# Two of the five passes of a weight conversion moved from VectorE to GpSimd, in a kernel of an mLSTM cell and a multiplicative feed-forward block

## Chip, cores, metric

One core of one Trainium2 chip. The metric is the time of one execution on the device in microseconds (us); of a kernel I give the median of its runs. All ratios below are of runs in the fast state; where a run fell in the slow state (a second state, with a time some per cent longer whatever the kernel) this is said.

## The reference, cut to what matters

```python
def _attn_ref(q, k, v, i_gate, f_gate, o_gate):      # batch 4, heads 8, seq 768, head_dim 40
    ...                                              # recurrent mLSTM cell, token by token
        C = f_stab[..] * C + i_stab[..] * einsum('bhd,bhe->bhde', vt, kt)
        h_tilde = einsum('bhde,bhe->bhd', C, qt)
        y[:, :, t] = o * h_tilde / maximum(abs(nq), 1.0)

def _moe_ref(x, w1, w2, w3, w_out):                  # 3072 tokens, d_model 320, d_ff 1024
    return (((x @ w1) * (x @ w2)) @ w3) @ w_out
```

The four weight matrices arrive as 64-bit floating-point numbers. The kernel loads them as pairs of 32-bit words and converts them itself on the way, while the cell runs. It folds `w3 @ w_out` into one matrix (`wp`, then `w3o`), for which each half of a 128-row block of `w3`, once converted, is transposed on VectorE.

## The kernel before

The main loop has 30 passes. Pass s computes chunk s of the cell, the `up` products (x times w1 and w2, tiles `pa` and `pb` in PSUM, the memory that TensorE writes to; their product, made by VectorE, is `ab`, which frees their bank of PSUM) of chunks already done, and later the `down` products (`po`). In the early passes it also converts weights. The parts that matter:

```python
    def to_f32(dst, raw):                       # one conversion: five passes on VectorE
        n = dst.shape[-1]                       # 512 columns, or 320 for w_out
        lo, hi = raw[:, :, 0], raw[:, :, 1]
        t = wst.tile([128, n], U32, name="ex", tag="ex", bufs=1)
        r = wst.tile([128, n], U32, name="ma", tag="ma", bufs=1)
        V = nc.vector
        V.tensor_scalar(out=t, in0=hi, scalar1=3, ... logical_shift_left)
        V.scalar_tensor_tensor(out=t, in0=hi, scalar=0x80000000, in1=t, ... and, or)
        V.tensor_scalar(out=r, in0=t, scalar1=0xFF800000, ... and)
        V.scalar_tensor_tensor(out=r.bitcast(FP), in0=lo, scalar=2.0 ** -52, in1=r.bitcast(FP), ... mult, mult)
        V.tensor_tensor(out=dst, in0=t.bitcast(FP), in1=r.bitcast(FP), op=OP.add)

    def twice(n):                               # the y copy: last columns of y, beside themselves
        nc.gpsimd.tensor_copy(out=y_t[n][:, DM:DM + REM], in_=y_t[n][:, KF * P:DM])

    def x_trans(n):                             # px: y transposed by TensorE, for up
        for cc in range(KF + 1):
            transpose(px[:, cc, :], y[:, cc * P:(cc + 1) * P])

    n_cvt = [2, 1, 1, 1, 2, 2, 3, 3, 3] + [2] * 7        # conversions of each pass
    for s in range(len(n_up)):
        ...
        if 0 <= s - 2 < NU:
            twice(s - 2)
        ...                                     # px, up, the cell (first VectorE instruction: L346), y
        for _ in range(n_cvt[s] if s < len(n_cvt) else 0):
            convert()                           # to_f32; for w3 also the VectorE transpose to w3T
```

Each engine works through its own list of instructions in order; the timelines below show it (a copy on GpSimd whose input is ready at 65.5 us runs at 74.18, after the four passes ahead of it in the list). A pass of the loop only says in which order they are issued.

## Time and profile before

| | before |
|---|---|
| median of 3 runs | 489.06 us (488.94 to 491.42) |
| profiled span | 486.4 us |
| TensorE, VectorE, ScalarE, GpSimd busy | 94%, 54%, 30%, 18% |
| mean granted TensorE clock (share of its full speed) | 0.98 |

In this document a **stretch** runs from one instruction L346 (L364 in the changed file) to the next, and has the number of the pass whose L346 ends it; stretch 5 (60.36 to 72.50 us) so holds the conversions that pass 4 issues. The prediction counts its steps this way too. It runs its step 7 up to the first `ab`, behind which TensorE resumes at 98.81 us ("15.0 today" after 83.82); its "step 8 … TensorE's 14 us" fits the time from there to the L346 at 113.04, and its step 9 runs from there (TensorE's wait for w3T ends at 128.59).

The timeline of GpSimd of the kernel before (start, length in us, engine, line, operation, output<-input, and in brackets the idle time before and who ended it):

```profile
63.94 0.47 POOL L305 TENSOR_TENSOR state<-state,decay 128x164 f32<-128x164 f32 x1
65.78 0.37 POOL L386 COPY y<-y 128x64 f32<-128x64 f32 x1 [1.38 <-DVE y L382]
73.50 0.46 POOL L305 TENSOR_TENSOR state<-state,decay 128x164 f32<-128x164 f32 x1 [7.35 <-DVE state L350]
```

GpSimd waits for y, copies its last columns at once, and then has nothing to do for 7.35 us. That gap is what the change wants to use. The groups of VectorE by shape (count, busy us, mean ns), for the two passes to be moved:

```profile
L188 DVE TENSOR_TENSOR w<-ex,ma 128x512 f32<-128x512 f32 x24 | 18.6, 777 | 0.7
L187 DVE SCALAR_TENSOR_TENSOR ma<-raw,ma 128x512 f32<-128x512 uint32 x24 | 17.6, 735 | 0.7
```

### The profile page before, as it was taken

What the parts mean: (1) busy time and instruction counts of PE and PEld (TensorE: products, weight loads), DVE (VectorE), ACT (ScalarE), POOL (GpSimd) and SP (SyncE); (2) the same over time, 40 slices, a digit from 0 to 9 for tenths busy, and PEclk for the clock granted to TensorE, in tenths of its full rate; (3) what the DMA queues carried; (4) which work ended last, traced back from release to release, by engine and by line L of the source; (5) the groups of instructions that cost most, each with busy time, mean ns of one, the idle gap of its engine ahead of it and who ended that gap; (6) DMA issues with size and microseconds to landing.
All of it is one profiled execution on the core that took longest, in us unless ns stands there. A gap on an engine that the chain in (4) does not pass through costs nothing.

```text
span 486.4 us, 13366 instructions
## 1 busy us (share of the span) xinstructions
PE 456.8 (94%) x5658; PEld 374.8 (77%) x5658; DVE 260.9 (54%) x526; ACT 146.6 (30%) x399; POOL 88.3 (18%) x165
## 2 busy tenths in 40 slices
PE   3879797989899999999999999999999998999997
PEld 2769696988687888888777787777877777778864
DVE  7797698999778878877460614515235033011110
ACT  3644453633442543434430312311101011011011
POOL 5431222711302321403220211101000000000000
PEclk9997998989999999999999999999999999999999
DMA  9999936789966847521551425234020000000001
GB/s 188 173 187 203 168 87 134 119 162 182 190 130 138 172 112 154 120 52 39 100 110 43 111 59 122 52 94 93 19 81 3 27 15 15 28 13 15 1 13 40
DMA packets 116187, 45.76 MB, mean 94 GB/s; under 512 B 96736, under 2 KB 107168, under 8 KB 116128
## 3 DMA queue, kind: packets, MB, share of 16 engines
q1 hardware_dynamic: 112528, 40.88, 42.2%
q10 hardware_dynamic: 3600, 4.03, 2.4%
q8 instruction: 44, 0.72, 0.7%
q14 instruction: 15, 0.12, 0.1%
HBM read 40.86 MB, written 4.03 MB: 92 GB/s over the span
## 4 chain that ended last, share of the span: by engine, by line
PE 75%; DVE 8%; issue 8%; DMA 4%; SPq 2%; POOL 2%; ACT 1%; POOLq 0%; DVEq 0%
PE po L90 21%; PE pa L90 21%; PE pb L90 14%; PE cell L90 8%; PE wp L90 7%; PE pt L93 2%; DVE h L370 2%; PE px L93 1%; SPq L168 1%; DMA raw<-in_moe_w_dram 1%; DMA kbuf<-in_k_dram 1%; PE ub L90 1%; DMA raw<-in_moe_w_out_dram 1%; DVE o_in L380 1%; POOL pw L278 1%
## 5 line engine op out<-in xcount | busy, mean ns | idle before, releaser
L542 DVE TENSOR_TENSOR ab<-pb,a_sb 128x512 f32<-128x512 f32 x48 | 33.0, 690 | 162.9 <-ACT a_sb L541 162.7
L90 PE MATMUL po<-w3o,ab 128*128 128x320 f32 x384 | 105.4, 433 | 1.3 <-DVE h L370 1.3
L90 PEld LDWEIGHTS po<-w3o,ab 128*128 128x128 f32 x384 | 72.2, 190 | 30.7 <-issue 1.5
L90 PE MATMUL pa<-xT,w 128*128 128x256 f32 (+1 forms) x448 | 94.6, 360 | 0.6 <-ACT xT L396 0.6
L90 PE MATMUL pb<-xT,w 128*128 128x256 f32 (+1 forms) x448 | 91.7, 350 | 0.3 <-issue 0.3
L90 PEld LDWEIGHTS pa<-xT,w 128*128 128x128 f32 x448 | 78.6, 200 | 11.7 <-ACT xT L396 1.0
L90 PEld LDWEIGHTS pb<-xT,w 128*128 128x128 f32 x448 | 76.1, 191 | 8.4
L541 ACT ACTIVATE a_sb<-pa 128x512 f32<-128x512 f32 x48 | 28.6, 596 | 147.9 <-PE pb L90 147.9
L90 PE MATMUL pb<-xT,wr 64*64 64x256 f32 (+1 forms) x448 | 47.5, 352 | 0.0
L90 PE MATMUL pa<-xT,wr 64*64 64x256 f32 (+1 forms) x448 | 47.5, 352 | 0.0
L305 POOL TENSOR_TENSOR state<-state,decay 128x164 f32<-128x164 f32 x40 | 19.6, 493 | 148.4 <-PE cell L90 94.0
L278 POOL TENSOR_SCALAR_AFFINE_SELECT pw<-pw 64x512 f32<-64x512 f32 x48 | 36.8, 768 | 47.0 <-ACT pw L276 45.4
L276 ACT ACTIVATE pw<-pw,aT 128x64 f32<-128x64 f32 x160 | 40.6, 339 | 10.5 <-DMA pw<-U_d 10.5
L90 PEld LDWEIGHTS pa<-xT,wr 64*64 64x64 f32 x448 | 28.5, 133 | 14.9 <-issue 6.8
L90 PE MATMUL wp<-wo,w3T 128*128 128x320 f32 x128 | 35.9, 433 | 2.0 <-DVE w3T L237 2.0
L90 PEld LDWEIGHTS wp<-wo,w3T 128*128 128x128 f32 x128 | 23.7, 190 | 11.1 <-issue 2.2
L90 PEld LDWEIGHTS cell<-vbuf,pw 64*64 64x64 f32 x768 | 27.4, 141 | 4.2 <-issue 2.0
L549 ACT COPY o_sb<-po 128x320 f32<-128x320 f32 x24 | 10.2, 425 | 67.6 <-PE po L90 66.7
L90 PE MATMUL cell<-vbuf,pw 64*64 64x41 f32 x768 | 27.3, 230 | 1.4 <-issue 1.4
L90 PEld LDWEIGHTS pb<-xT,wr 64*64 64x64 f32 x448 | 28.5, 133 | 0.0
L386 POOL COPY y<-y 128x64 f32<-128x64 f32 x24 | 7.3, 302 | 109.9 <-DVE y L382 106.1
L346 DVE TENSOR_TENSOR pw<-cell,pw 128x512 f32<-128x512 f32 x24 | 16.4, 685 | 17.2 <-PE cell L90 13.6
(89 smaller groups left out, 514.3 us busy)
## 6 DMA issues: line engine op xcount, KB each, us to landing
raw<-in_moe_w_dram SPq DMA_DIRECT2D x64, 128.0 KB, 3.2
pw<-U_d SPq DMA_DIRECT2D x40, 128.0 KB, 3.6
kbuf<-in_k_dram SPq DMA_DIRECT2D x24, 160.0 KB, 4.5
vbuf<-in_v_dram SPq DMA_DIRECT2D x24, 160.0 KB, 4.9
o_in<-in_o_gate_dram SPq DMA_DIRECT2D x24, 160.0 KB, 3.9
out_dram<-o_sb ACTq DMA_DIRECT2D x24, 160.0 KB, 1.8
raw<-in_moe_w_dram SPq DMA_DIRECT2D x7, 512.0 KB, 6.0
qbuf<-in_q_dram SPq DMA_DIRECT2D x17, 160.0 KB, 5.1
```

Of the source, the lines that this page charges most:

```text
L90: in_order(nc.tensor.matmul(out, lhsT=lhsT, rhs=rhs, start=start, stop=stop))
L93: in_order(nc.tensor.transpose(out, in_, ident[0:n, 0:n]))
L168: nc.sync.dma_start(out=dst, in_=src)
L276: nc.scalar.activation(out=pw[:, h, :], in_=src[:, h, :], func=AF.Exp, bias=aT[:, c, b * H + h:b * H + h + 1])
L278: nc.gpsimd.affine_select(out=pw[r], in_=pw[r], compare_op=OP.is_ge, fill=0.0, base=0, pattern=[[0, H], [1, L]], channel_multiplier=-1)
L305: nc.gpsimd.tensor_tensor(out=new, in0=old, op=OP.mult, in1=decay[:, b * NP:(b + 1) * NP, 2 * c + x:2 * c + x + 1] .to_broadcast([P, NP, D1]))
L346: first_read = nc.vector.tensor_tensor(out=pv, in0=ss, in1=pv, op=OP.mult)
L370: nc.vector.tensor_tensor(out=h[r], in0=ph[x], in1=h[r], op=OP.add)
L386: nc.gpsimd.tensor_copy(out=y_t[n][:, DM:DM + REM], in_=y_t[n][:, KF * P:DM])
L541: nc.scalar.mul(out=a_sb, in_=pa, mul=UP ** -2)
L542: nc.vector.tensor_tensor(out=ab_t[gr][j][:, fs[0]:fs[-1] + 1, t0:t0 + a_sb.shape[-1]], in0=pb, in1=a_sb, op=OP.mult)
L549: nc.scalar.copy(out=o_sb, in_=po)
```

## The change

The intent: VectorE is about 90% busy in stretches 5 to 9 and GpSimd is not, so the multiply and the add that end a conversion go to GpSimd. The multiply on GpSimd is a plain one, so ScalarE scales the low words first. The scratch of such a conversion lies in `gates`, a tile that is free by then, one pair of columns for all. The transposes of w3 are put off to the next pass (`unturned`), so that VectorE needn't wait for GpSimd at once. Of the 34 conversions, the last two of each of passes 4 to 14 are changed, 22 in all.

```diff
-    def to_f32(dst, raw):
+    def to_f32(dst, raw, E=None):
...
+        if E is None:
+            t, r = (tiles "ex", "ma" as before)
+        else:
+            t, r = (gates[:, i * CW:i * CW + n].bitcast(U32) for i in range(2))
...
+        if E is None:
             V.scalar_tensor_tensor(out=r.bitcast(FP), in0=lo, scalar=2.0 ** -52, in1=r.bitcast(FP), op0=OP.mult, op1=OP.mult)
+        else:
+            V = E
+            nc.scalar.mul(out=lo.bitcast(FP), in_=lo, mul=2.0 ** -52)
+            V.tensor_tensor(out=r.bitcast(FP), in0=lo.bitcast(FP), in1=r.bitcast(FP), op=OP.mult)
         V.tensor_tensor(out=dst, in0=t.bitcast(FP), in1=r.bitcast(FP), op=OP.add)
...                                    # convert(): the transpose of w3 becomes turn_w3()
+        if E is None:
+            turn_w3(w3, ko, half)
+        else:
+            unturned.append((w3, ko, half))
...                                    # main loop
-            weighted(s)
-            if s >= B:
-                decayed(state[s % B][1], state[s % B][0], s, 0)
+            if s <= early:
+                weigh(s)
...
-        for _ in range(n_cvt[s] if s < len(n_cvt) else 0):
-            convert()
+        if early <= s < NU - 1:
+            weigh(s + 1)
+        while unturned:
+            turn_w3(*unturned.pop(0))
+        for i in range(n_cvt[s] if s < len(n_cvt) else 0):
+            convert(nc.gpsimd if i + 2 >= n_cvt[s] and early <= s < len(n_cvt) - 1 else None)
```

`early` is 4; `weigh` holds the two lines that were taken out above. In the changed file L184 to L186 are L187 to L189, the multiply is L191 on VectorE and L195 on GpSimd, the add L196, the scaling on ScalarE L194, the y copy L404, the transpose to w3T L254, `ab` L560.

More of the change, by code (lines that the diff above doesn't have):

```diff
@@ L173, in scale @@
         nc.scalar.mul(out=hi, in_=hi, mul=2.0 ** -111)
-    def to_f32(dst, raw):
+    def to_f32(dst, raw, E=None):
         n = dst.shape[-1]
         lo, hi = raw[:, :, 0], raw[:, :, 1]
-        t = wst.tile([128, n], U32, name="ex", tag="ex", bufs=1)
-        r = wst.tile([128, n], U32, name="ma", tag="ma", bufs=1)
+        if E is None:
+            t = wst.tile([128, n], U32, name="ex", tag="ex", bufs=1)
+            r = wst.tile([128, n], U32, name="ma", tag="ma", bufs=1)
+        else:
+            t, r = (gates[:, i * CW:i * CW + n].bitcast(U32) for i in range(2))
         V = nc.vector
@@ L186, in to_f32 @@
         V.tensor_scalar(out=r, in0=t, scalar1=0xFF800000, scalar2=None, op0=OP.bitwise_and)
-        V.scalar_tensor_tensor(out=r.bitcast(FP), in0=lo, scalar=2.0 ** -52, in1=r.bitcast(FP), op0=OP.mult, op1=OP.mult)
+        if E is None:
+            V.scalar_tensor_tensor(out=r.bitcast(FP), in0=lo, scalar=2.0 ** -52, in1=r.bitcast(FP), op0=OP.mult, op1=OP.mult)
+        else:
+            V = E
+            nc.scalar.mul(out=lo.bitcast(FP), in_=lo, mul=2.0 ** -52)
+            V.tensor_tensor(out=r.bitcast(FP), in0=lo.bitcast(FP), in1=r.bitcast(FP), op=OP.mult)
         V.tensor_tensor(out=dst, in0=t.bitcast(FP), in1=r.bitcast(FP), op=OP.add)
@@ L224, in scale_next, with convert @@
         scale(scaled[-1][1])
-    def convert():
+    def convert(E=None):
         if not scaled:
@@ L230, in convert, with turn_w3 @@
         if dst is not None:
-            to_f32(dst, raw)
+            to_f32(dst, raw, E)
             return
         w3 = wst.tile([128, CW], FP, name="w3", tag="w3")
-        to_f32(w3, raw)
-        if half == 0:
+        to_f32(w3, raw, E)
+        if ko not in w3T_t:
             w3T_t[ko] = wst.tile([128, FO, 128], FP, name="w3T", tag="w3T")
+        if E is None:
+            turn_w3(w3, ko, half)
+        else:
+            unturned.append((w3, ko, half))
+    unturned, halves_in = [], {}
+    def turn_w3(w3, ko, half):
         nc.vector.transpose(out=w3T_t[ko].rearrange("c k (m r) -> c m k r", r=32)[:, 2 * half:2 * half + 2],
                             in_=w3.rearrange("r (m k c) -> r m k c", m=2, k=FO))
-        if half:
+        halves_in[ko] = halves_in.get(ko, 0) + 1
+        if halves_in[ko] == 2:
             turned_w3.append(ko)
@@ L562, with weigh @@
     n_cvt = [2, 1, 1, 1, 2, 2, 3, 3, 3] + [2] * 7
-    pinned = 7
+    pinned, early = 7, 4
     behind = ExitStack()
     turned, converted, fetched = 0, 2, 2 * KF + 1
+    def weigh(n):
+        weighted(n)
+        if n >= B:
+            decayed(state[n % B][1], state[n % B][0], n, 0)
     for s in range(len(n_up)):
```

## The prediction

> **What bounds the kernel now.** A step is one pass of the main loop (s = 0 to 29). I read four views, from coarse to fine: the busy table and chain of the page, the stretch table cut at the starts of the step's first VectorE instruction (L346, `pw<-cell`), the waits of TensorE, and the timelines of the steps that the change touches.
>
> ```profile
> PE 456.8 (94%) x5658; PEld 374.8 (77%) x5658; DVE 260.9 (54%) x526; ACT 146.6 (30%) x399; POOL 88.3 (18%) x165
> ...
> PE 75%; DVE 8%; issue 8%; DMA 4%; SPq 2%; POOL 2%; ACT 1%; POOLq 0%; DVEq 0%
> ```
>
> TensorE is the bound on the whole and GpSimd is mostly idle. The averages hide two stages.
>
> ```profile
> 60.36:72.50 12.14, 12.14 (x227) 11.62 (x227) 10.95 (x22) 6.42 (x17) 3.25 (x6) 0.92 0.36 87
> 72.50:83.82 11.32, 8.02 (x184) 7.37 (x184) 10.12 (x23) 4.13 (x13) 3.25 (x6) 0.85 0.72 139
> 83.82:101.44 17.62, 15.36 (x285) 14.94 (x283) 16.06 (x34) 10.04 (x29) 8.97 (x14) 0.96 0.67 127
> 101.44:113.04 11.60, 11.60 (x251) 11.41 (x251) 10.74 (x26) 3.89 (x12) 3.65 (x6) 0.92 0.97 183
> 113.04:127.14 14.10, 13.57 (x214) 11.64 (x211) 13.11 (x28) 6.84 (x18) 2.64 (x5) 1.00 0.94 190
> 128.59:486.40 357.81, 352.86 (x3616) 278.81 (x3616) 153.44 (x304) 85.70 (x221) 43.37 (x75) 1.00 0.31 69
> ```
>
> The columns are length, then busy PE, PEld, DVE, ACT, POOL, then clock. The first five rows are steps 5 to 9: VectorE is busy about 90%, and it sets the pace together with TensorE. The last row is everything after: TensorE is busy without a break, VectorE 43%. The chain of waits says the same: from 128.59 us on it is nearly all matmuls. So VectorE time is worth something only before 128.6 us. A gain there is capped by what TensorE waits for:
>
> ```profile
> PE px L93 <- DVE y L382: 3.8, 2, 3.3
> PE cell L90 <- POOL vw L300: 2.6, 2, 1.9
> PE pt L93 <- DVE ab L542: 2.3, 1, 2.3
> PE wp L90 <- DVE w3T L237: 2.0, 1, 2.0
> ```
>
> Of these px, pt and wp, some 8 us or 1.6%, lie in the changed steps. A gain over 2% is therefore hardly possible.
>
> **What the Trainium skill says.** "GPSIMD Engine Reference", section "Performance versus the Vector engine", gives about 2.6 cycles per element at 1.2 GHz for a two-input operation on GpSimd and calls it about twice as slow as VectorE. The trace has two sizes of such an operation (with a broadcast second operand):
>
> ```profile
> 61.37 0.47 POOL L305 TENSOR_TENSOR state<-state,decay 128x164 f32<-128x164 f32 x1 [7.78 <-DVE state L350]
> 63.24 0.74 POOL L300 TENSOR_TENSOR vw<-vbuf,wT 128x328 f32<-128x328 f32 x1
> ```
>
> The columns are start and length in us: 0.47 and 0.74 us (465 and 737 ns as medians), a slope of 1.66 ns per element, so 1.04 us for 512 elements; the page's figure gives 1.1 us plus the 0.19 us intercept of my line, 1.3. I take 1.2 us for 128x512 and 0.8 us for 128x320, as estimates. "TensorE: Matmul & The Clock Gate", Part 1, says that an idle window of about 3.4 us halves the matmul clock until about 3.4 us of work have passed. The trace agrees: in step 6 TensorE waits 3.31 us for y and then runs at half clock:
>
> ```profile
> 79.50:80.50 1.00, 1.00 (x26) 0.50 0.00 0
> 80.50:81.50 1.00, 1.00 (x32) 0.50 0.28 77
> 81.50:82.50 1.00, 1.00 (x50) 0.50 0.62 183
> ```
>
> **The change part by part.** 22 of 34 conversions (the last two of each of steps 4 to 14, two being all there are except in steps 6 to 8) move their last two passes. VectorE loses 2 x 0.69 us for each 128x512 and 2 x 0.49 for each 128x320 one, about 28 us in all: plenty, but 12 x 1.38 = 17 us of it after step 9, where it has time anyway. ScalarE gains 22 scalings of the low words (0.68 or 0.50 us, some 14 us; it is 30% busy, so I charge nothing). GpSimd gains 44 operations, some 49 us on 88. The matmuls are the same, but the first product of w3 moves from step 10 to step 11 and step 17 does two.
>
> What decides is the order. Reading the built program with its semaphores, three things stand out.
> 1. The pair of scratch tiles (in `gates`) is single. The first VectorE pass of a step's second conversion waits for the GpSimd add of the first. VectorE then stands still, in order, where it used to go on.
> 2. GpSimd's small copy of y's last columns (L386 before) now stands behind both conversions of the step before. In steps 5 and 6, where one `up` is done, TensorE's px of the step needs that copy, and behind px stand the rest of `up` and all cell matmuls, in order.
> 3. From step 8 on px is of the y one step older, so the copy has a whole step of slack. But the transposes of w3 on VectorE wait for GpSimd's add, ahead of `ab`.
>
> Today the stretch that this lengthens is:
>
> ```profile
> 65.22 0.49 DVE L382 TENSOR_TENSOR y<-h,o_in 128x320 f32<-128x320 f32 x1
> 65.63 0.42 DVE L184 TENSOR_SCALAR ex<-raw 128x512 uint32<-128x512 uint32 x1
> ...
> 66.81 0.43 DVE L186 TENSOR_SCALAR ma<-ex 128x512 uint32<-128x512 uint32 x1
> 67.28 0.69 DVE L187 SCALAR_TENSOR_TENSOR ma<-raw,ma 128x512 f32<-128x512 uint32 x1
> ...
> 72.50 0.68 DVE L346 TENSOR_TENSOR pw<-cell,pw 128x512 f32<-128x512 f32 x1
> ```
>
> y is done at 65.71, the y copy at 66.15, px follows at once, and the cell matmuls end at 69.88; VectorE is the later one, with its two conversions until 71.86.
>
> Step 5, new: three passes until 67.24; GpSimd 2 x 1.2 until 69.7; three passes (1.55) until 71.3; GpSimd until 73.8; y copy 0.25, 74.1. TensorE has idled some 7.5 us and starts at half clock, so from the copy to the end of the cell matmuls I take what step 6 shows today in that state, 78.28 to 83.57, 5.3 us. L346 at 79.4 instead of 72.50: **+6.9**.
> Step 6, new: y is ready 5.35 us after L346, at 84.75; three passes, GpSimd 2.4, three passes of 128x320 (1.2), GpSimd 1.6, handovers 0.2: 91.7; copy, 91.95; 5.3 more: 97.25 instead of 83.82. A further **+6.5**.
> Step 7 needs no new px. From L346 to the first `ab` (which frees TensorE's PSUM bank): 5.35 + 2.5 (a whole conversion) + 1.2 + 1.65 (wait for GpSimd) + 1.2 + 1.2 + 0.65 = 13.75 us against 15.0 today: **-1.2**. Step 8 is then TensorE's 14 us as today.
> Step 9: VectorE from L346: y with three passes and a wait within, 7; wait and transpose, 1.5; three passes 1.6; GpSimd 2.5; transpose 0.7; two `ab` 1.4: 14.7 us, 2.2 more than TensorE's work, so TensorE resumes at 14.75 after the cell matmuls. Today it resumes at 15.8, after its wait of 2.0 for w3T, which is gone: **-1.1 to -1.3**, the product of w3 itself being paid later.
> From step 10 a step is 16.8 us of matmuls; VectorE needs some 14 and GpSimd 3.4 + 2 x 2.4 = 8.2, so nothing further. Sum: 6.9 + 6.5 - 1.2 - 1.3 = +10.9, **500.0 us**, 2.2% slower.
>
> **The rivals.** (a) The intended gain: VectorE's relief lets steps 5 to 9 shrink to TensorE's work, 3 to 8 us, 481 to 486 us. For it: VectorE is 90% busy there and L346 of step 5 comes 2.6 us after its matmuls. Against it: the two waits above are in the program, not guesses. (b) A wash: the early loss is smaller, because GpSimd takes 1.04 us or less and the clock falls for one step only; then the sum is +6 to +8, 495 to 497 us. For it: step 7 was stretched by DMA and GpSimd at the same time, and gives some back. (c) Worse: GpSimd and VectorE slow each other. Today L188 has a mean of 777 ns against a minimum of 678, L278 768 against 652. GpSimd at 1.5 us adds 0.3 to each of eight operations in steps 5 and 6, and its late release of raw buffers holds the queue of loads: 503 to 508.
>
> **Range and chances.** I take 500 us. The range 492 to 508 runs from the wash to the worse rival with one more us to spare at the low end for step 7. The 2% line is at 498.8, just under my value, so slower 0.55, same 0.42; faster 0.03, as even all the waits together hold no 2%.
>
> **What would show it.** Right: a TensorE wait `px <- POOL y` of some 7 us twice, near 66 to 74 and 84 to 92 us; clock near 0.5 after each; VectorE idle before the first pass of second conversions until GpSimd's add; L346 of step 6 near 97; the wait of wp for w3T gone; matmuls unbroken from about 140 us and then as today. Wrong: px starting without waiting on GpSimd, L346 of step 6 before 90 (GpSimd's passes well under 1 us, or y copied earlier), or new TensorE waits after step 10 (then slower still).

## The result, and the profile after

| | before | changed |
|---|---|---|
| median (runs of the same rounds) | 490.24 us (4 runs, 488.94 to 493.24) | 512.10 us (4 runs, 509.07 to 513.54) |
| ratio, 95% interval | | 1.0429 [1.0352, 1.0505] |
| profiled span | 486.4 us | 507.4 us |
| mean granted clock | 0.98 | 0.96 |

A ratio here is the mean time of one kernel's fast runs over that of the other's of the same rounds, so not quite the ratio of the medians. The change makes the kernel 4.3% slower: the direction was predicted, but the time is 4 us above the top of the range.

The busy times and the chain of work that ended last, from the page of the changed kernel:

```profile
PE 460.1 (91%) x5658; PEld 375.7 (74%) x5658; DVE 237.2 (47%) x482; ACT 158.4 (31%) x421; POOL 135.4 (27%) x209
...
PE 68%; POOL 5%; issue 5%; DVE 4%; DMA 2%; ACT 1%; SPq 1%; POOLq 0%; DVEq 0%; ACTq 0%
```

VectorE lost 23.7 us of work, GpSimd gained 47.1, as meant. But GpSimd's share of the chain rose from 2% to 5%. The stretches 5 to 9, in the order length, busy PE, PEld, DVE, ACT, POOL, clock:

```profile
60.19:79.88 19.69, 10.31 (x204) 9.62 (x204) 8.24 (x18) 5.27 (x16) 8.16 (x10) 0.74 0.64 115
79.88:99.75 19.87, 11.64 (x204) 10.90 (x204) 7.85 (x18) 7.52 (x21) 7.35 (x10) 0.71 0.45 81
99.75:118.00 18.25, 16.49 (x288) 15.82 (x289) 14.98 (x33) 12.46 (x39) 10.59 (x16) 0.94 0.40 83
118.00:130.97 12.97, 11.73 (x257) 11.07 (x255) 10.12 (x23) 5.49 (x13) 8.65 (x13) 1.00 0.94 187
130.97:145.43 14.46, 12.43 (x200) 10.50 (x201) 11.00 (x23) 5.08 (x14) 7.93 (x9) 1.00 0.83 173
```

In stretches 5 and 6 TensorE is busy for 52% and 59% of the time, and at a clock of 0.74 and 0.71. What it waits for (us in all, times, longest):

```profile
PE px L93 <- POOL y L404: 15.6, 2, 8.4
...
PE pt L93 <- DVE ab L560: 4.2, 5, 1.9
...
PE px L93 <- DVE y L400: 2.7, 3, 1.0
PE pa L90 <- DVE ab L560: 1.8, 2, 0.9
...
PE wp L90 <- DVE ab L560: 0.7, 1, 0.7
```

The wait of `wp` for w3T is gone, as predicted, and the one `px <- POOL y` is there twice, as predicted. Of the waits for `ab`, 6.7 us in all, the prediction had one, of 2.2 us in its step 9 (1.90 measured, below). The others were not predicted, and three of them (0.68, 0.62 and 0.29 us, at 177 to 212 us) lie after step 10, which the prediction named as a sign that it was wrong. GpSimd in stretch 5, which answers to the timeline shown of before:

```profile
67.20 1.29 POOL L195 TENSOR_TENSOR gates<-raw,gates 128x512 f32<-128x512 f32 x1 [2.97 <-issue]
68.56 1.26 POOL L196 TENSOR_TENSOR w<-gates 128x512 f32<-128x512 f32 x1
71.61 1.29 POOL L195 TENSOR_TENSOR gates<-raw,gates 128x512 f32<-128x512 f32 x1 [1.78 <-issue]
72.97 1.26 POOL L196 TENSOR_TENSOR w<-gates 128x512 f32<-128x512 f32 x1
74.18 0.24 POOL L404 COPY y<-y 128x64 f32<-128x64 f32 x1
```

y was done at 65.5 us (L400 on VectorE), and its copy starts at 74.18, where before it followed within 0.1 us: it stands behind four passes in GpSimd's list. Between the two conversions VectorE stands still as well, because there is one pair of scratch tiles (VectorE of the changed kernel):

```profile
66.64 0.43 DVE L189 TENSOR_SCALAR gates<-gates 128x512 uint32<-128x512 uint32 x1
69.86 0.43 DVE L187 TENSOR_SCALAR gates<-raw 128x512 uint32<-128x512 uint32 x1 [2.79 <-POOL w L196]
...
79.88 0.69 DVE L364 TENSOR_TENSOR pw<-cell,pw 128x512 f32<-128x512 f32 x1 [1.65 <-PE cell L90]
```

**Where the 21 us are.** Each row is the difference of the stretches' lengths between the two traces, taken from the starts of L346 and L364. From the end of stretch 17 (270.06 us before, 290.81 after) both kernels take 20.2 us a stretch.

| stretches | before | after | difference | predicted |
|---|---|---|---|---|
| start of stretch 5 | 60.36 | 60.19 | -0.17 | 0 |
| 5 | 12.14 | 19.69 | +7.55 | +6.9 |
| 6 | 11.32 | 19.87 | +8.55 | +6.5 |
| 7 and 8 | 29.22 | 31.22 | +2.00 | -1.2 |
| 9 to 17 | 157.02 | 159.84 | +2.82 | -1.3 |
| sum | | | +20.75 | +10.9 |

In the last row lies a shift that is no loss: the product of w3 of stretch 10 is done one stretch later, and so on until stretch 17 does two (260 matmuls instead of 244, 28.82 us instead of 24.51). The loss in it begins at the end of stretch 9 (VectorE of the changed kernel):

```profile
140.23 0.43 DVE L189 TENSOR_SCALAR gates<-gates 128x512 uint32<-128x512 uint32 x1
143.48 0.71 DVE L254 STREAM_TRANSPOSE w3T<-w 128x512 f32<-128x512 f32 x1 [2.82 <-POOL w L196]
144.22 1.29 DVE L560 TENSOR_TENSOR ab<-pb,a_sb 128x512 f32<-128x512 f32 x2
```

The second transpose of w3 waits 2.82 us for GpSimd's add, and `ab` stands behind it in VectorE's list. TensorE needs the PSUM bank that `ab` frees. It waits 1.90 us for it, where the prediction had 2.2, and then works at half clock, which the prediction didn't have (TensorE, then two slices of one microsecond with busy PE, PEld, DVE, ACT, POOL and clock):

```profile
144.97 0.66 PE L93 MATMUL pt<-ident,qbuf 128*128 128x128 f32 x4 [1.90 <-DVE ab L560]
```

```profile
147.00:148.00 1.00, 1.00 (x4) 0.82 (x3) 0.97 (x3) 1.00 (x3) 0.00 (x0) 0.50 0.82 240
148.00:149.00 1.00, 1.00 (x3) 0.80 (x3) 0.92 (x4) 0.85 (x2) 0.00 (x0) 0.50 0.47 121
```

This adds up. TensorE's idle time in stretches 9 to 13 is 0.53 + 1.89 = 2.42 us before and 2.03 + 0.68 + 0.62 + 0.30 = 3.63 us after (length minus busy in each stretch), 1.2 us more; the last three are again waits for `ab`. Stretch 10 has a mean clock of 0.89, so 0.11 x 15.32 = 1.7 us of it are lost to the clock. Together 2.9 us, against 2.82.

**GpSimd and VectorE get in each other's way.** In the same stretch two passes of VectorE that take 0.49 us elsewhere took 1.23 and 1.44 us, beside passes of GpSimd (VectorE, then GpSimd):

```profile
135.83 1.23 DVE L398 SCALAR_TENSOR_TENSOR o_in<-o_in,den 128x320 f32<-128x320 f32 x1
137.10 1.44 DVE L400 TENSOR_TENSOR y<-h,o_in 128x320 f32<-128x320 f32 x1
```

```profile
135.41 1.30 POOL L195 TENSOR_TENSOR gates<-raw,gates 128x512 f32<-128x512 f32 x1 [2.88 <-DMA raw<-in_moe_w_dram]
136.79 1.40 POOL L196 TENSOR_TENSOR w<-gates 128x512 f32<-128x512 f32 x1
```

Each of the two ends 0.35 us after the GpSimd pass beside it ends (137.06 against 136.71, 138.54 against 138.19). This is what the Trainium skill says in "SBUF — State Buffer", section "SBUF: two separate sides": VectorE's second pair of ports is shared with GpSimd as an exclusive lock, which a VectorE operation with two SBUF inputs and a GpSimd operation that reads SBUF take one after the other. The trace agrees; VectorE's two passes are 0.74 + 0.95 = 1.7 us longer here.

**Half clock lasts longer.** In stretch 6 the y copy ends at 92.98 us, and the cell matmuls at 99.68, 6.7 us later. The prediction took 5.3, from a stretch in which the half clock lasted some 3.4 us. Slices of the changed kernel:

```profile
93.00:94.00 1.00, 0.97 (x13) 0.74 (x17) 0.00 (x0) 0.45 (x1) 0.00 (x0) 0.50 1.29 227
...
97.00:98.00 1.00, 1.00 (x49) 1.00 (x46) 0.00 (x0) 1.00 (x6) 0.00 (x0) 0.50 1.01 208
...
101.00:102.00 1.00, 1.00 (x6) 1.00 (x5) 0.73 (x2) 0.73 (x2) 0.94 (x3) 0.51 0.00 0
102.00:103.00 1.00, 1.00 (x10) 1.00 (x10) 0.96 (x2) 1.00 (x5) 0.92 (x2) 1.00 0.00 0
```

TensorE is busy from 93.0 on, but the full clock comes back only at 102.0, after 9 us of work. In stretch 5 of the same kernel it came back after 3.6 us. Nor did the half clock always need the idle 3.4 us that the prediction took: it followed waits of TensorE of 1.90 us (above), of 2.26 us in the kernel before (98.81 us; clock 0.50 from 100 to 103) and of 1.98 us in e5 (129.72 us; 0.50 from 131 to 133), but not the wait of 1.98 us at 128.59 us in the kernel before (1.00 in the slices behind it). So none of the traces gives a fixed length of wait.

### The profile page after: what moved, and what is told of

It is laid out like the page before. It is cut to its first block, busy times and chain, and to the rows that moved or that the text cites. A ratio compares the mean times of both kernels' runs of the same rounds, so it can differ in the third digit from the quotient of the medians.

```text
span 507.4 us, 13428 instructions
## 1 busy us (share of the span) xinstructions
PE 460.1 (91%) x5658; PEld 375.7 (74%) x5658; DVE 237.2 (47%) x482; ACT 158.4 (31%) x421; POOL 135.4 (27%) x209
## 4 chain that ended last, share of the span: by engine, by line
PE 68%; POOL 5%; issue 5%; DVE 4%; DMA 2%; ACT 1%; SPq 1%; POOLq 0%; DVEq 0%; ACTq 0%
PE po L90 20%; PE pa L90 19%; PE pb L90 13%; PE cell L90 7%; PE wp L90 6%; POOL gates L195 2%; PE pt L93 2%; PE px L93 1%; DMA raw<-in_moe_w_out_dram 1%; DMA qbuf<-in_q_dram 1%; ACT pw L294 1%; POOL w L196 1%; SPq L168 1%; POOL pw L296 1%; DVE h L388 1%
## 5 line engine op out<-in xcount | busy, mean ns | idle before, releaser
L560 DVE TENSOR_TENSOR ab<-pb,a_sb 128x512 f32<-128x512 f32 x48 | 32.8, 689 | 168.9 <-ACT a_sb L559 168.6
L90 PE MATMUL pb<-xT,w 128*128 128x256 f32 (+1 forms) x448 | 92.8, 353 | 0.2 <-issue 0.2
L90 PEld LDWEIGHTS pb<-xT,w 128*128 128x128 f32 x448 | 77.3, 195 | 8.5
L323 POOL TENSOR_TENSOR state<-state,decay 128x164 f32<-128x164 f32 x40 | 19.2, 485 | 112.7 <-PE cell L90 65.5
L90 PE MATMUL pa<-xT,wr 64*64 64x256 f32 (+1 forms) x448 | 49.1, 362 | 0.0
L90 PE MATMUL pb<-xT,wr 64*64 64x256 f32 (+1 forms) x448 | 49.1, 362 | 0.0
L90 PEld LDWEIGHTS pa<-xT,wr 64*64 64x64 f32 x448 | 29.9, 139 | 15.1 <-issue 7.2
L195 POOL TENSOR_TENSOR gates<-raw,gates 128x512 f32<-128x512 f32 (+1 forms) x22 | 26.6, 1209 | 52.8 <-DVE gates L189 17.6
L296 POOL TENSOR_SCALAR_AFFINE_SELECT pw<-pw 64x512 f32<-64x512 f32 x48 | 33.3, 694 | 25.4 <-ACT pw L294 23.7
L93 PE MATMUL px<-ident,y 128*128 128x128 f32 x72 | 13.9, 295 | 18.3 <-POOL y L404 15.6
L90 PEld LDWEIGHTS pb<-xT,wr 64*64 64x64 f32 x448 | 29.9, 139 | 0.0
L404 POOL COPY y<-y 128x64 f32<-128x64 f32 x24 | 6.6, 275 | 86.8 <-DVE y L400 86.5
```

What stands on the lines that cost most here:

```text
L90: in_order(nc.tensor.matmul(out, lhsT=lhsT, rhs=rhs, start=start, stop=stop))
L93: in_order(nc.tensor.transpose(out, in_, ident[0:n, 0:n]))
L195: V.tensor_tensor(out=r.bitcast(FP), in0=lo.bitcast(FP), in1=r.bitcast(FP), op=OP.mult)
L296: nc.gpsimd.affine_select(out=pw[r], in_=pw[r], compare_op=OP.is_ge, fill=0.0, base=0, pattern=[[0, H], [1, L]], channel_multiplier=-1)
L323: nc.gpsimd.tensor_tensor(out=new, in0=old, op=OP.mult, in1=decay[:, b * NP:(b + 1) * NP, 2 * c + x:2 * c + x + 1] .to_broadcast([P, NP, D1]))
L560: nc.vector.tensor_tensor(out=ab_t[gr][j][:, fs[0]:fs[-1] + 1, t0:t0 + a_sb.shape[-1]], in0=pb, in1=a_sb, op=OP.mult)
```

## The experiments

The theory after reading the result: A, the y copy behind GpSimd's conversion passes makes most of the loss (stretches 5 and 6). Rivals and additions: B, the single pair of scratch tiles, which makes VectorE and GpSimd take turns; the order of the loop, which was changed as well; the half clock; and the transposes of w3 that wait for GpSimd ahead of `ab`. The expectations name theories by such letters; those of the last four runs are explained there. All twelve runs computed the right result.

| kernel | median us (runs) | ratio to before, 95% |
|---|---|---|
| changed | 512.10 (4) | 1.0429 [1.0352, 1.0505] |
| e1_ycopy | 498.85 (4) | 1.0197 [1.0113, 1.0281] |
| e2_scratch | 508.41 (4) | 1.0414 [1.0337, 1.0491] |
| e3_both | 497.07 (4) | 1.0180 [1.0105, 1.0254] |
| e4_none | 491.01 (4) | 1.0073 [0.9979, 1.0167] |
| e5_late | 495.85 (6) | 1.0110 [1.0080, 1.0141] |
| e6_warm | 509.41 (4) | 1.0396 [1.0354, 1.0439] |
| e7_no_w3 | 491.31 (6) | 1.0009 [0.9971, 1.0046] |
| e8_one_no_w3 | 491.14 (6) | 1.0007 [0.9976, 1.0038] |
| e9_both_gated | 490.24 (6) | 1.0025 [0.9968, 1.0083] |
| e10_late_gated | 489.72 (6) | 1.0044 [0.9962, 1.0126] |
| e11_vw_first | 490.23 (6) | 0.9997 [0.9939, 1.0054] |
| e12_one_gated | 494.65 (6) | 1.0109 [1.0059, 1.0158] |

The kernel before had medians of 489.0 to 490.8 us in these rounds, which ran on several chips; each ratio is to the kernel before of its own round. One run of it (493.15 us) and one of e11 were slow and are left out of the ratios.

### e1: the y copy ahead of the conversions

```diff
-        if 0 <= s - 2 < NU:
+        if 0 <= s - 2 < NU and (s - 2 < early - 1 or s - 1 > NU):
             twice(s - 2)
...
         if early <= s < NU - 1:
             weigh(s + 1)
+        if early <= s <= NU:
+            twice(s - 1)
```

> The changed kernel, but GpSimd's copy of y's last columns is issued ahead of the two conversions of its step instead of behind them. Theory A (the copy stuck behind the conversions makes most of the loss, through px and all that stands behind it on TensorE): the waits of px for GpSimd (8.4 and 7.2 us) go, step 5 and step 6 return to about 12 us each (19.7 and 19.9 in the changed kernel), VectorE's first instruction of step 6 starts near 84 to 86 us instead of 99.75, and the time falls by about 15 us to 493 to 498. Rival B (GpSimd's slow passes and the handovers with VectorE over the one pair of scratch tiles cost it, wherever the copy stands): steps 5 and 6 stay above 16 us and less than 6 us are saved.

Measured: 498.85 us, 1.0197. Stretches 5 and 6 are 11.96 and 12.64 us instead of 19.69 and 19.87, and no `px` waits for GpSimd any more. The time is 0.85 us above the expected range. GpSimd in stretch 5:

```profile
67.24 0.37 POOL L404 COPY y<-y 128x64 f32<-128x64 f32 x1 [1.38 <-DVE y L400]
68.84 1.30 POOL L195 TENSOR_TENSOR gates<-raw,gates 128x512 f32<-128x512 f32 x1 [1.23 <-DVE gates L189]
```

So the place of one instruction of 0.3 us in GpSimd's list makes more than half of the loss (1.0429 to 1.0197), as A said. The GpSimd passes themselves are as long as in the changed kernel, and stretch 5 is no longer than before the change (11.96 against 12.14 us).

### e2: a second pair of scratch tiles

```diff
-        if E is None:
+        if E is None or flip:                  # flip: the last conversion of a pass uses "ex", "ma"
             t = wst.tile([128, n], U32, name="ex", tag="ex", bufs=1)
```

> The changed kernel, but the last conversion of a step uses the other pair of scratch tiles, so VectorE no longer waits for GpSimd's add before its second conversion; the copy of y stays behind the conversions. Theory A: GpSimd's four passes stand back to back, so the copy comes some 1.7 us earlier in steps 5 and 6 and VectorE's 2 us wait in step 7 goes: 4 to 6 us less than the changed kernel, 505 to 508. Rival B (the single pair of scratch tiles is the main cause): 10 us or more less, below 502.

Measured: 508.41 us, 1.0414; its interval covers that of the changed kernel nearly whole. The waits `px <- POOL y` fell from 15.6 to 12.3 us, so the taking of turns makes some 3 us of the wait, not the wait. The gain of 3.7 us is a little under the 4 to 6 expected. B falls as the main cause.

### e3: both

The edits of e1 and e2 together.

> Both mends together: copy of y ahead of the conversions, second pair of scratch tiles. Theory A: steps 5 and 6 as in the kernel before or 1 to 2 us shorter, the rest of the changed kernel's loss (some 5 us from step 7 on, by the step starts) partly kept: 488 to 494. Rival C (GpSimd's contention with VectorE and the later w3 products are a large loss by themselves): above 498.

Measured: 497.07 us, 1.0180. It is slower than expected: 1.8% are left, and they lie elsewhere, since stretches 5 to 7 are now 10.98, 11.73 and 17.07 us, together 1.3 us shorter than before. The waits of TensorE point to `ab` (all three lie between 109 and 163 us, in stretches that convert on GpSimd):

```profile
PE pt L93 <- DVE ab L560: 7.2, 3, 3.8
```

### e4: the order of the changed loop, with all conversions on VectorE

```diff
-            convert(nc.gpsimd if i + 2 >= n_cvt[s] and early <= s < len(n_cvt) - 1 else None)
+            convert(None)
```

> The loop order of the changed kernel (products of the next step's weights a step earlier) with all conversions on VectorE again and nothing moved to GpSimd or ScalarE. Theory A: the order alone costs nothing, within 1% of the kernel before, 487 to 493. Rival D (the new place of GpSimd's weighting, not the conversions, costs the time): above 498.

Measured: 491.01 us, 1.0073 with an interval that holds 1. The order alone costs nothing that is clear; the interval reaches to 1.7%, but e7 and e9 below keep this order, beside other edits, and stay under 1%.

### e5: only the conversions of w3 from pass 9 on

```diff
-            ... and early <= s < len(n_cvt) - 1 else None)
+            ... and 9 <= s < len(n_cvt) - 1 else None)
```

> The changed kernel with only the conversions of w3 from step 9 to 14 (12 of the 22) on GpSimd; steps 4 to 8 convert on VectorE alone. Theory A with its third part (from step 9 on VectorE's transposes of w3 wait for GpSimd's adds ahead of the products ab, which frees TensorE's banks late, and one product of w3 moves to step 17): step starts up to step 9 as in the kernel before, step 17 starts 3 to 7 us later; 493 to 497. Rival E (late steps have slack, as the prediction said; the whole loss is in steps 5 to 8): within 2 us of the kernel before, 488 to 492.

Measured: 495.85 us, 1.0110 [1.0080, 1.0141]. The stretches up to 9 are as before, and the loss is there all the same: stretch 17 ends at 277.52 instead of 270.06 us, 6.3 us more after the 1.1 us that this run was late at stretch 9. Waits of TensorE and of VectorE:

```profile
PE pt L93 <- DVE ab L560: 4.8, 5, 2.6
```

```profile
DVE w3T L254 <- POOL w L196: 18.0, 7, 2.8
```

The first line must be read with care: its longest wait, 2.6 us, lies at 100 us, where the kernel before has one of 2.3 us too. From stretch 10 on this trace has waits for `ab` of 2.9 us together (five, the longest 1.09 us), and stretch 10 has a clock of 0.92, which loses some 1.5 us. That is 4.4 of the 6.3 us; the trace doesn't show where the rest is. So the late part of the change, which the prediction took for free, loses about 1% by itself.

### e6: TensorE kept warm while it waits

```diff
         for cc in range(KF + 1):
+            for _ in range(44 if cc == KF and n in (3, 4) else 0):
+                transpose(px[:, cc, :], y[:, 0:P])
             transpose(px[:, cc, :], y[:, cc * P:(cc + 1) * P])
```

The extra transposes write what the last one overwrites, and fill most of the wait for the y copy with work (of the 15.6 us of `px <- POOL y` 4.8 are left).

> The changed kernel with 44 transposes of 128x128 that nothing reads (they are overwritten by the real one) put on TensorE between the second and third block of px in steps 5 and 6, so that TensorE is busy while it waits for GpSimd's copy. Theory A with the clock part (after an idle 7 to 8 us TensorE runs at half clock and the cell matmuls take 5.4 and 6.7 us from the copy instead of some 3.7): the granted clock of steps 5 and 6 rises from 0.74 and 0.71 to above 0.9, the stretch from the copy to the end of the cell matmuls falls to 3.7 to 4.2 us, and the time falls by 3 to 6 us, 506 to 509. Rival F (the clock is no part of the loss): same time, within 1 us, or longer.

Measured: 509.41 us, 1.0396; the interval overlaps that of the changed kernel. In the trace stretch 6 kept a clock of 1.00 instead of 0.71 and took 18.30 instead of 19.87 us; stretch 5 was as long as without (19.65), at a clock of 0.78 where above 0.9 was expected: it was at half clock until 67 us and again from 77 to 81. The half clock is so worth some 1.6 us in stretch 6; on the whole time the run is inconclusive.

### e7 and e8: both mends, and GpSimd only for passes 4 to 7

```diff
-            ... if i + 2 >= n_cvt[s] and early <= s < len(n_cvt) - 1 else None, flip=(i + 1 == n_cvt[s]))
+            ... if i + 2 >= n_cvt[s] and early <= s < 8 else None, flip=(i + 1 == n_cvt[s]))     # e7
+            ... if i + 1 >= n_cvt[s] and early <= s < 8 else None, flip=(i + 1 == n_cvt[s]))     # e8
```

> Copy of y ahead, second scratch pair, and only the conversions of steps 4 to 7 (7 or 8 of them, none of w3) on GpSimd. Theory A with its third part: what is left of the loss of the kernel with both mends (about 1.8%) was from the w3 conversions, so this is at or a little below the kernel before, 484 to 490, with TensorE unbroken from step 10 on as before. Rival G (GpSimd's contention in steps 4 to 8 is the remainder): 494 or more.

> As the kernel with only the conversions of steps 4 to 7, but only the last one of each step on GpSimd. If GpSimd's share in steps 5 to 8 is too large with two per step (state decay behind 5 us of passes holding VectorE's h), this is 1 to 3 us faster than with two, 483 to 488; if VectorE's relief is what counts, 1 to 3 us slower. Against the kernel before: at most 8 us faster, as that is all TensorE waits there.

Measured: 491.31 and 491.14 us, 1.0009 and 1.0007, both the same as before within 0.5%. Without the w3 conversions the loss is gone, with eight or with four conversions on GpSimd. But there is no gain either, and both are above the times expected. (e8 has the fault of edit that is told under e12, but VectorE waits only 1.4 us for it there.) In e7 the wait of `wp` for w3T, 2.0 us before, is 3.6 us: TensorE comes sooner to the first product of w3 and finds it not ready.

### e9 and e10: the transposes of w3 behind the next y

```diff
-        while unturned:
-            turn_w3(*unturned.pop(0))
+        with tc.issue_after(gated.ins) if gated else nullcontext():     # gated: the y of this pass
+            while unturned:
+                turn_w3(*unturned.pop(0))
```

e10 adds this to e5, e9 adds it to e3. The transposes so come behind both `ab` of the pass that converted, and by then GpSimd's add is done.

> As e5_late (GpSimd only for the w3 conversions of steps 9 to 14, which measured 1.011 of the kernel before), but the transposes of a converted w3 half are put behind the y of the next step in VectorE's order, and so behind the two ab of the step that converted it. Theory D (the 1% of e5_late is TensorE waiting for ab, which stood behind a transpose that waits for GpSimd): the waits pt <- ab of 4.8 us go, and with them the half clock after them; 489 to 492 us, ratio 0.995 to 1.005. Rival E (the 1% is the longer instructions on VectorE beside GpSimd, or the product of w3 that stands one step later and doubles in step 17): 494 to 497 us, ratio 1.008 to 1.014, with step 17 still starting near 277.5. Rival F: the wait only moves, from pt for ab to wp for w3T, near 3 to 5 us; then 492 to 495.

> As e3_both (copy of y ahead of the conversions and a second pair of scratch tiles; it measured 1.018 of the kernel before), with the transposes behind the y of the next step as in e10_late_gated. Theory D: pt <- ab (7.2 us in e3_both) goes, 487 to 492 us, ratio 0.995 to 1.005, about what e7_no_w3 gave (1.0009). Rival E or F: 494 to 498 us. Should it come under 484 us the whole idea of the change would pay after all; I give that 3 in 100, as TensorE's own work from step 10 on is the same.

Measured: e10 489.72 us, 1.0044; e9 490.24 us, 1.0025. The intervals of e3 and e9 don't overlap (nor do the ranges of runs of e5, 494.64 to 497.22, and e10, 487.25 to 493.76), so the order of transpose and `ab` is the cause of the late loss. (The intervals of e5 and e10 do overlap; these two ran on different chips.) VectorE waits for GpSimd's adds nearly as long in e10 (15.9 us in 11 waits, now at the next conversion) as in e5 (18.0 us in 7), so not the length of the waiting made the loss, but what stood behind it. In e10 no TensorE wait for `ab` is left in the changed stretches; its one wait for `ab`, 3.9 us, lies before 99 us, where its conversions are still all on VectorE. The end of stretch 17 is 270.83 us in e10 and 270.48 in e9, with 28.82 us for stretch 17 in both: the later product of w3 costs nothing, and the contention of VectorE and GpSimd, which e9 still has, costs nothing that shows in the time (what VectorE is relieved of may hide it). The waits of e9:

```profile
PE cell L90 <- POOL vw L318: 6.8, 4, 2.7
PE px L93 <- DVE y L400: 5.0, 3, 3.5
...
PE pt L93 <- DVE ab L560: 0.7, 1, 0.7
```

So the change can be made harmless with all its 22 conversions. It still gains nothing. In the trace of e9 stretch 9 ends 4.0 us sooner than before (123.18 against 127.14 us). But 2.7 of these were there when stretch 5 began (57.67 against 60.36), before anything runs on GpSimd in place of VectorE; the other traces begin stretch 5 anywhere from 59.96 to 63.15. Stretches 5 to 9 themselves take 65.51 us against 66.78, so VectorE's relief is worth at most 1.3 us there, and that isn't clear of the spread: e4, e5 and e10, which convert on VectorE alone in these stretches, take 68.08, 66.72 and 67.53 us. A part of the relief is lost because the engines slow each other: with the same 482 instructions VectorE is busy for 253.3 us in e9 and 237.2 in the changed kernel (260.9 before), so of 23.7 us less work only 7.6 are left. Beside GpSimd's passes at 148 to 152 us below, VectorE's L188 and L189 took 1.68 and 2.00 us, where they take 0.69 and 0.43 just before. The lead is given back later: stretch 17 ends 0.4 us later than before. In between TensorE waits once 2.72 us for `vw`, and has a clock of 0.90 in stretches 11 and 12, which loses 0.1 x (17.48 + 18.34) = 3.6 us. That wait is again one of GpSimd's list (GpSimd, then TensorE):

```profile
148.40 1.37 POOL L195 TENSOR_TENSOR gates<-raw,gates 128x512 f32<-128x512 f32 x1 [2.54 <-DMA raw<-in_moe_w_dram]
149.71 1.11 POOL L296 TENSOR_SCALAR_AFFINE_SELECT pw<-pw 64x512 f32<-64x512 f32 x1
150.80 1.26 POOL L196 TENSOR_TENSOR w<-gates 128x512 f32<-128x512 f32 x1
152.13 0.73 POOL L296 TENSOR_SCALAR_AFFINE_SELECT pw<-pw 64x512 f32<-64x512 f32 x1
152.94 0.78 POOL L318 TENSOR_TENSOR vw<-vbuf,wT 128x328 f32<-128x328 f32 x1
```

```profile
153.78 1.09 PE L90 MATMUL cell<-vw,kbuf 64*64 64x41 f32 x32 [2.72 <-POOL vw L318]
```

### e11 and e12: `vw` ahead of the masks; one conversion a pass

```diff
+        if early <= s < NU - 1:
+            weigh(s + 1)
         if B - 1 <= s < NU:
             if s + 1 < NU:
                 weights(s + 1)
...
-        if early <= s < NU - 1:
-            weigh(s + 1)
```

e11 adds this to e9; e12 adds it too, and takes `i + 1 >= n_cvt[s]`, one conversion a pass.

> As e9_both_gated (1.0025 of before), but vw of the next step is issued to GpSimd ahead of the masks of pw of the next step, so it no longer stands behind a conversion pass and the two masks. In e9 the 4 us won by stretch 9 (123.18 against 127.14) went to one wait cell <- vw of 2.72 us near 151 to 154 and the half clock of some 6 us behind it. Theory D2 (that wait and its clock are what ate the gain): the wait cell <- vw falls from 6.8 to under 3 us, the clock of stretches 11 and 12 is 1.00, and the time is 484 to 487 us, ratio 0.987 to 0.994. Rival G (TensorE is fed by several queues at once, and the wait goes to pt <- ab, px <- y or pw): 488 to 491, ratio 0.997 to 1.003. I give D2 40 in 100.

> As e11_vw_first, but only the last conversion of each step has its two passes on GpSimd, 11 in place of 22: half of what the change adds to GpSimd, and no VectorE wait for the single pair of scratch tiles inside a step. If GpSimd's own load, in order, is what eats the gain, this is the faster of the two by 1 to 3 us (483 to 487); if VectorE's relief were worth more, it is slower than e11 by as much. If TensorE's own work bounds both, both are within 1 us of each other at 486 to 491.

Measured: e11 490.23 us (one of its six runs slow), 0.9997: no gain. The number is that of rival G, but it doesn't test what it was to test. In its trace the 2.7 us wait for `vw` is still there, and GpSimd's order around it is that of e9: the edit moved `vw` in other passes and not in this one. (The profiled run is the slow one; I take only the order from it.) Whether these last us can be had stays open. Its expectation also counted all of the 4 us by which e9 led as won by the change, where at most 1.3 were.

e12: 494.65 us, 1.0109, 4.4 us slower than e11 with half of GpSimd's load; the expectation allowed for 1 to 3 us slower, but for another reason (less relief of VectorE). Its trace suggests why, and it is a fault of my edit that repeats the finding; no run without the fault was made. With one conversion a pass the GpSimd one uses the tiles `ex` and `ma`, and so does the VectorE one after it. VectorE waits in its list for GpSimd's add, ahead of `ab` (VectorE of e12, then TensorE):

```profile
157.80 0.85 DVE L187 TENSOR_SCALAR ex<-raw 128x512 uint32<-128x512 uint32 x1 [2.82 <-POOL w L196]
158.68 1.01 DVE L188 SCALAR_TENSOR_TENSOR ex<-raw,ex 128x512 uint32<-128x512 uint32 x1
159.72 0.69 DVE L560 TENSOR_TENSOR ab<-pb,a_sb 128x512 f32<-128x512 f32 x1
```

```profile
160.47 1.12 PE L93 MATMUL pt<-ident,qbuf 128*128 128x128 f32 x4 [2.93 <-DVE ab L560]
```

The same 2.82 us, by a scratch tile this time instead of a transpose, and again a loss of about 1%.

## Why the prediction was right and wrong

The direction, the main wait and its place were foretold. The sum, +10.9 us, was short by 9.9: by 2.7 in stretches 5 and 6, 3.2 in 7 and 8, 4.1 from 9 on. The first is a matter of sizes; in the other two a step of the reasoning failed.

- **No gain to be had: right as far as tried.** TensorE is 94% busy, and even the mended forms (e7 to e11) stay within 0.5% of the kernel before.
- **The y copy behind the conversions, +6.9 and +6.5 us: the mechanism right, the size too small by 2.7 us** (measured +7.55 and +8.55). e1 takes it away and stretches 5 and 6 are short again. Two terms of the sum were mis-sized. GpSimd's pass was taken as 1.2 us for 128x512 and 0.8 for 128x320 and took 1.30 and 0.88, some 0.4 us in each stretch. I had two figures, 1.04 and 1.3, and split the difference, where the one worked out with the skill's 2.6 cycles was right. And from the copy to the end of the cell matmuls I took 5.3 us, which stretch 5 kept (5.4) and stretch 6 didn't (6.7), as the half clock lasted 9 us there instead of 3.4. e6 shows that this is worth about 1.6 us.
- **Stretches 7 and 8, -1.2 us: wrong by 3.2 us; the steps that failed are a conversion's VectorE passes at their usual length, and step 8 as TensorE's own 14 us.** "Step 7 needs no new px" was right, and VectorE's wait for GpSimd was 1.99 us against 1.65. But the first `ab` let TensorE resume 14.9 us after L364 (114.68 against 99.75) and not 13.75. VectorE works without a break from its wait to that `ab`, and its last three passes before it, taken as 1.2 us, took 2.4: beside GpSimd, L188 and L189 (111.89 and 113.02 us) took 1.09 and 0.88 us, where the same passes take 0.49 and 0.33 elsewhere in that stretch. From there to the next L364 it took 16.3 us and not 14: VectorE stands 2.50 us for GpSimd's add (at 121.40), which the prediction left out, and TensorE waits three times more for `ab` (0.87, 0.46 and, up to 131.10 us, 0.91 us). No run separates these 2 us further.
- **From stretch 9 on, -1.3 us: wrong by 4.1 us; the step that failed is "from step 10 … so nothing further".** I compared busy times, VectorE's 14 us and GpSimd's 8.2 us in a stretch of 16.8, and took the slack for room. Step 9 itself, with the wait for GpSimd's add ahead of `ab` in its sum, was nearly right: TensorE resumed 14.0 us after L364 (144.97 against 130.97; predicted 14.75; the sum took -1.3 for it, where 14.75 against 15.8 is -1.05). What I left out is that the clock falls behind this wait too, and that the same order stands in the later passes: 1.7 us were lost to half clock right behind the wait, and 1.6 us in three more waits for `ab` up to stretch 13. That is 3.3 of the 4.1 us. A VectorE that is idle for a third of these stretches still delays TensorE, if its idle time lies in front of `ab`. e5 shows the loss alone, and e10 and e9 take it away by order alone; in the trace of e12 another wait at the same place goes with a loss again.
- **Rival (a), the gain:** the relief is small (at most 1.3 us in stretches 5 to 9 of e9). In the trace it is gone again behind the wait for `vw`; no run shows what the time is without that wait.
- **Rival (b), a smaller early loss with GpSimd at 1.04 us or less:** GpSimd took 1.30 us, and the early loss was larger, not smaller.
- **Rival (c), GpSimd and VectorE slow each other:** seen in the trace, and it made the last passes of step 7 longer, but e9 has more of it and loses nothing clear, so it isn't the cause of the 4%. The same holds for VectorE's longest new wait, that of the state for GpSimd's decay (24.2 us in 19 waits, 11.4 before): e9 has 22.2 us of it. Its figure, 503 to 508 us for GpSimd passes of 1.5 us, came nearest, by luck: the passes took 1.30 us.

The parts roughly add up: the copy 2.3% (the changed kernel to e1), the scratch 0.2%, which the intervals don't separate from zero (e1 to e3), the transposes 1.6% (e3 to e9), and nothing clear left. They can't be read off the table of stretches, though: the copy's wait hid part of the other loss. Without it TensorE waits longer for `ab` (`pt <- DVE ab` is 4.2 us in the changed kernel, 6.7 in e1 and 7.2 in e3).

## What to carry to other kernels

When a pass moves to an idle engine, look first at what stands behind it in that engine's list, and at what stands behind the wait for it in the list of the engine it left. Here both lists held a small instruction that the bounding engine needs: a copy of 0.3 us, and an `ab` of 0.7 us. Slack in a stretch's busy time says nothing of this, and both losses went by a change of order, not of load.

## What the Trainium skill lacked or had wrong

- "TensorE: Matmul & The Clock Gate", Part 1, "What's actually happening", has the full clock come back after at least one busy window of some 3.4 us. It did after 3.6 us in stretch 5 of the changed kernel (granted clock 0.95 from 78.0 us on, the copy's end at 74.42), but only after 9 us in stretch 6 (half clock from 93.0 to 102.0 us with TensorE busy in each slice). Why is open. Half clock also followed waits of 1.90, 1.98 and 2.26 us, shorter than the idle 3.4 us that the prediction takes from the same part.
- "GPSIMD Engine Reference", section "Performance versus the Vector engine": its 2.6 cycles per element fit. The two sizes measured, 1.306 and 0.880 us for 512 and 320 elements, give a slope of 2.22 ns, which is 2.66 cycles at the page's 1.2 GHz. It has no figure for an operation with a broadcast second operand; the two sizes that the prediction shows give 1.66 ns per element.
- "SBUF — State Buffer", section "SBUF: two separate sides": the exclusive lock agrees (0.49 us passes that took 1.23 and 1.44 us, each ending 0.35 us after the GpSimd pass beside it). The factors that the page gives are of other operations; here a block cost 0.74 and 0.95 us for a pass.
- The table at the head of "TensorE: Matmul & The Clock Gate" calls the queues of ScalarE, VectorE and GpSimd strict FIFOs, but no page that I read draws the consequence that cost most here: a 0.24 us copy behind four passes of GpSimd kept TensorE waiting for 8.38 and 7.24 us, and that is 2.3 of the 4.3% (the changed kernel against e1).
